# Weight strips and residual tiles moved in two transfers, partitions 0 to 119 and 120 to 127

## The chip, the cores and the metric

The kernel runs on one core of one Trainium2 chip. The metric is the device time of one execution in microseconds (us), as the median of several runs. The profile comes from one further execution, recorded by the hardware profiler. Its engines are TensorE (PE, with its weight loads shown apart as PEld), VectorE (DVE), ScalarE (ACT), GpSimd (POOL) and SyncE (SP), which here issues nearly all data transfers (DMA). A line such as L507 is a line of the kernel.

## The reference, cut to what matters

Four layers in a row on 2048 tokens of width 576: A, B, A, B, each added to its input (the residual) after a layernorm. A is a local attention over 8 dilated positions, with a product with `wqkv` before it and one with `wo` behind it. B is a recurrent attention: it goes through the tokens in segments of 32, and each segment also sees 8 memory rows that the segment before it produced.

```python
def _A_ref(x, wqkv, wo):
    W, dil = (8, 2)                                   # 32 heads of 18
    qkv = ...(x @ wqkv)...
    idx = pos[:, None] - (jnp.arange(W) * dil)[None, :]
    ...                                               # softmax over the 8 positions, times v
    return o @ wo

def _B_ref(x, mem0, Wq, Wk, Wv, Wo, seg_len):         # 32 heads of 128
    mem = mem0
    for s in range(n_seg):                            # 64 segments of 32 tokens
        h = jnp.concatenate([mem, xs], axis=1)
        q, k, v = ...                                 # h times Wq, Wk, Wv
        ...                                           # masked softmax, times v, times Wo
        mem = o[:, :M, :].copy()                      # the next segment needs it
        outs.append(o[:, M:, :])

x = x + _A_ref(_layernorm(x), A_wqkv, A_wo)
x = x + _B_ref(_layernorm(x), B_mem0, B_Wq, B_Wk, B_Wv, B_Wo, B_seg_len)
x = x + _A_ref(_layernorm(x), A_wqkv, A_wo)
x = x + _B_ref(_layernorm(x), B_mem0, B_Wq, B_Wk, B_Wv, B_Wo, B_seg_len)
```

All inputs are bfloat16.

## The kernel before

All four layers run interleaved: while the two B layers (two "lanes", five segments apart) step through their segments, the two A layers work on tiles of 64 tokens ahead of them. A small planner inside the kernel orders the work of every engine when the program is built; its estimates, and not the chip, decide the order. B's weights (`wq`, `wk`, `wv`, `wo`) stay in on-chip memory. A's weights don't fit beside them. They are cut into 12 strips (9 of `wqkv`, 3 of `wo`), and each tile of A fetches all 12 in turn into a ring of three buffers:

```python
self.strips = [dp.tile([P, 5 * 256], BF16, name=f"strip{i}") for i in range(12)]   # in DRAM
tiles("ring", 3, [P, 5 * 256])                                                     # on chip

def wload(self, i, src, rows, col0, n, prio, dep):
    ...
    def fetch(e):
        dma(out=w.t[:, 0:5 * n], in_=self.strips[i][:, 0:5 * n])
    ...
    o = pl.op("SP", 0.9 if k <= COPY else 0.5, gather if k <= COPY else fetch, prio,
              [dep, self.strip_in.get(i)], acq=[w], lat=4.0)
    if k == COPY:     # the third use also writes the packed strip to DRAM, for the later fetches
        self.strip_in[i] = pl.op("SP", 0.5, lambda e: dma(out=self.strips[i][:, 0:5 * n],
                                                          in_=w.t[:, 0:5 * n]), prio, [o], uses=[w])
```

Two of three strips have n = 256 (128 partitions of 2560 bytes, 320 KB), the third has n = 128 (160 KB). A strip's buffer is taken again when TensorE has read it. TensorE reads it here (L570 for `wqkv`, L680 for `wo`), one weight load and one matmul for each of 25 pieces of three strips:

```python
nc.tensor.matmul(ps.t[:, c * T:(c + 1) * T], lhsT=view()[:, kc, w0:w0 + P], rhs=xn.t[:, kc, :],
                 start=(kc == 0), stop=(kc == 4))
```

The output of each A tile, which B's result is added to later, goes to DRAM (L689) and comes back when B reaches it (L715); a tile is 128 partitions of 1280 bytes:

```python
nc.sync.dma_start(out=(self.x1T if layer == 1 else self.x3T)[:, j], in_=xT.t[:])   # store
nc.sync.dma_start(out=b.t[:], in_=src[:, j])                                       # load again
```

The rest of TensorE's work is B: projections to q and k (L832, L835), v (L879), scores (L919 to L929), probabilities times v (L970) and the product with `wo` (L994):

```python
for h in range(4 * k, 4 * k + 4):
    for mb in range(5):
        nc.tensor.matmul(psY.t[...], lhsT=self.wo[:, w0:w0 + P], rhs=self.OT[:, ..., c0:c1], ...)   # L994
```

Of the kernel before, what the change touches and what calls it, by code (L numbers as in the profile page):

```python
# [35 lines left out]
EPS = 1e-5  # L36
NQ = T // 16
CB = (0, 126, 252, 378, 448)


class _Buf:
# [206 lines left out]
class _K:  # L248
# [37 lines left out]
    def setup(self):  # L286
# [19 lines left out]
        nc.gpsimd.memset(epad[:], 1.0)  # L306
        for t_, pat, b0 in ((epad[:, 0:4, :], [[CB[1], 4]], 0), (epad[:, 4, :], [], CB[4])):
            self.sel(t_, pat + [[-AD, AH]], 1, b0, ALU.is_ge, 0.0)
            self.sel(t_, [[-a, n] for a, n in pat] + [[AD, AH]], -1, AD - 1 - b0, ALU.is_ge, 0.0)
        self.sel(epad[:, 0:4, :], [[0, 4], [0, AH]], -1, HPC * AD - 1, ALU.is_ge, 0.0)  # L310
        self.sel(epad[:, 4, :], [[0, AH]], 1, CB[4] - 4 * HPC * AD, ALU.is_ge, 0.0)
        self.epadT = epadT = cp.tile([P, 5, P], BF16, name="epadT")
        et = epadT[0:AH]
        nc.gpsimd.memset(et, 1.0)
        for t_, pat, b0 in ((et[:, 0:4, :], [[CB[1], 4]], 0), (et[:, 4, :], [], CB[4])):
            self.sel(t_, pat + [[1, P]], -AD, b0, ALU.is_ge, 0.0)
            self.sel(t_, [[-a, n] for a, n in pat] + [[-1, P]], AD, AD - 1 - b0, ALU.is_ge, 0.0)
        nc.gpsimd.memset(et[:, 0:4, HPC * AD:P], 0.0)
        nc.gpsimd.memset(et[:, 4, 0:4 * HPC * AD - CB[4]], 0.0)
        self.ma0 = ma0 = cp.tile([AH, AW, 16], F32, name="ma0")  # L320
# [168 lines left out]
    def wload(self, i, src, rows, col0, n, prio, dep):  # L489

        pl, dma = self.pl, self.nc.sync.dma_start
        step, last = rows
        self.strip_n[i] = k = self.strip_n.get(i, -1) + 1
        w = pl.buf("ring") if k else None

        def view():
            return (w.t if k else self.wo[:, i * 1280:(i + 1) * 1280])[:, 0:5 * n].rearrange("p (k n) -> p k n", k=5)

        def gather(e):
            f, v, r, m = src[0:1, col0:col0 + 1], view(), min(P, src.shape[0] - last), min(n, src.shape[1] - col0)
            dma(out=v[:, 0:4, 0:m], in_=bass.AP(f.tensor, f.offset, [[src.shape[1], P], [step * src.shape[1], 4], [1, m]]))
            (dma if k else self.nc.scalar.dma_start)(out=v[0:r, 4, 0:m], in_=src[last:last + r, col0:col0 + m])

        def fetch(e):
            dma(out=w.t[:, 0:5 * n], in_=self.strips[i][:, 0:5 * n])  # L507
        if k == 0:
            o = self.first = pl.op("SP", 0.65, gather, -20.0 + 0.01 * i, lat=4.0)
            return view, (), o  # L510
        o = pl.op("SP", 0.9 if k <= COPY else 0.5, gather if k <= COPY else fetch, prio, [dep, self.strip_in.get(i)], acq=[w], lat=4.0)
        if k == COPY:
            self.strip_in[i] = pl.op("SP", 0.5, lambda e: dma(out=self.strips[i][:, 0:5 * n], in_=w.t[:, 0:5 * n]), prio, [o], uses=[w])
        return view, (w,), o

    def a_tile(self, layer, j, dep, due, span):

        nc, pl = self.nc, self.pl
# [3 lines left out]
        def pr(f):  # L522
            return due - span * (1.0 - f)
        Q = PR[f"A{layer}"]
        if layer == 1:
            xT = pl.buf("x1")
# [8 lines left out]
            b = pl.op("PE", 0.16, tr, pr(0.04), [a], acq=[ps, xT], uses=[x0], mm=5)  # L535
            o_x = pl.op(AD_, _evac(320), lambda e, ps=ps: self.copy(e, xT.t[:], ps.t[:, 0:5 * T].rearrange("p (c t) -> p c t", c=5)),
                        pr(0.05), [b], uses=[ps, xT])
        else:
            xT = self.acc[0][j][0]
# [19 lines left out]
        for part in (0, 1, 2):  # L559
            ps = pl.buf("r")  # L560
            o = o_n
            for c in range(5):
                if c % 2 == 0:
                    n = 256 if c < 4 else P
                    view, w, ow = self.wload(part * 3 + c // 2, self.A_wqkv, (P, 512), part * D + CB[c], n, pr(Q[1]) - PR[f"ring{layer}"], wgate)
                w0 = c % 2 * CB[1]

                def mm(e, c=c, view=view, ps=ps, w0=w0):
                    for kc in range(5):
                        nc.tensor.matmul(ps.t[:, c * T:(c + 1) * T], lhsT=view()[:, kc, w0:w0 + P], rhs=xn.t[:, kc, :],  # L570
                                         start=(kc == 0), stop=(kc == 4))
                o = pl.op("PE", 0.146, mm, pr(Q[1] + 0.03 * part), [o, ow], acq=[ps, dst[part]] if c == 0 else (),
                          uses=[xn, *w] if c == 0 else [xn, *w, ps], lat=0.0 if c < 4 else None, mm=5)
                if c == 0 and part > 0:
                    def hcopy(e, part=part):
# [3 lines left out]
                        else:  # L579
                            self.copy(e, h, hin[0].t[:, part - 1])  # L580
                    got[part, "h"] = pl.op("DVE" if first else ("POOL", "ACT") if early else "POOL", 0.25, hcopy, pr(Q[1]), [o] if first else [o, hin[1]],
                                           uses=[dst[part]] if first else [dst[part], hin[0]])
# [22 lines left out]
        o = None  # L605
        for n, (c0, nb) in enumerate(((0, 2), (2, 2), (4, 1))):
            def prod(e, c0=c0, nb=nb):
                self.tt(e, big.t[:, c0:c0 + nb], qT.t[:, c0:c0 + nb].unsqueeze(2).to_broadcast([P, nb, AW, T]),
                        win(kT.t, c0, nb), ALU.mult)
            o = pl.op(("POOL", "DVE") if early else "POOL", (1.0 * nb + 0.05, 0.15 + 0.3 * nb), prod, pr(Q[2] + 0.02 * n), [o] if o else [got[0], got[1], got[1, "h"]],  # L610
                      acq=[big] if n == 0 else (), uses=[qT, kT] if n == 0 else [big, qT, kT], lk=True)
# [9 lines left out]
        o = o_l = pl.op("PE", 0.29, logits, pr(Q[3]), [o], acq=[psL, e_], uses=[big], mode="C", mm=20)  # L621

        def amax(e):
            v = psL.t[:, 0:P].rearrange("p (w t) -> p w t", w=AW)
            if first:
# [3 lines left out]
        o = pl.op("DVE", 0.6, amax, pr(Q[3]), [o], acq=[nmx], uses=[psL])  # L629
        o = pl.op("ACT", 0.28, lambda e: nc.scalar.activation(out=e_.t[:], in_=psL.t[:, 0:P].rearrange("p (w t) -> p w t", w=AW),  # L630
                                                              func=ACT.Exp), pr(Q[3]), [o], uses=[psL, e_])

        def norm(e):
            nc.vector.tensor_reduce(out=ssum.t[:], in_=e_.t[:].rearrange("p w t -> p t w"), axis=AX.X, op=ALU.add)
            nc.vector.reciprocal(out=ssum.t[:], in_=ssum.t[:])
        o = pl.op("DVE", 0.68, norm, pr(Q[3]), [o], acq=[ssum], uses=[e_])
        o = pl.op("DVE", 0.3, lambda e: self.tt(e, e_.t[:], e_.t[:], ssum.t[:].unsqueeze(1).to_broadcast([P, AW, 16]), ALU.mult),
                  pr(Q[3]), [o], uses=[e_, ssum], lk=True)

        def spread(ps, c0, nb):  # L640
            for c in range(nb):
                for g in range(NQ):
                    q4 = slice(g * AH, (g + 1) * AH)
                    nc.tensor.matmul(ps[g].t[:, c * P:(c + 1) * P], lhsT=self.epadT[q4, c0 + c, :],  # L644
                                     rhs=e_.t[q4].rearrange("p w t -> p (w t)"), start=True, stop=True, skip_group_check=True)
        b = o
        evs = {}
        for n, (c0, nb) in enumerate(((0, 2), (2, 3))):
            ps = [pl.buf("r") for _ in range(NQ)]
            b = pl.op("PE", 0.03 + 0.05 * nb, lambda e, ps=ps, c0=c0, nb=nb: spread(ps, c0, nb), pr(Q[4] + 0.02 * n), [b], acq=ps,  # L650
                      uses=[e_], mode="R", mm=4 * nb)
# [6 lines left out]
        for c0, nb in ((0, 2), (2, 2), (4, 1)):  # L658
# [6 lines left out]
        o = pl.op(PD, (2.6, 0.85), lambda e: self.tt(e, big.t[:, :, 0:4], big.t[:, :, 0:4], big.t[:, :, 4:8], ALU.add),  # L665
                  pr(Q[5] + 0.02), mus, uses=[big], lk=True)
        o = pl.op(PD, (1.44, 0.5), lambda e: self.tt(e, big.t[:, :, 0:2], big.t[:, :, 0:2], big.t[:, :, 2:4], ALU.add),
                  pr(Q[5] + 0.04), [o], uses=[big], lk=True)
        o = o_o = pl.op(PD, (0.78, 0.33), lambda e: self.tt(e, oT.t[:], big.t[:, :, 0], big.t[:, :, 1], ALU.add),
                        pr(Q[5] + 0.06), [o], acq=[oT], uses=[big], lk=True)  # L670
        ps = pl.buf("r")
        for mb in range(5):
            if mb % 2 == 0:
                n = 256 if mb < 4 else P
                view, w, ow = self.wload(9 + mb // 2, self.A_wo, (CB[1], CB[4]), mb * P, n, pr(Q[6]) - PR[f"ring{layer}"], o_l)
            w0 = mb % 2 * P

            def mm(e, mb=mb, view=view, ps=ps, w0=w0):
                for c in range(5):
                    nc.tensor.matmul(ps.t[:, mb * T:(mb + 1) * T], lhsT=view()[:, c, w0:w0 + P], rhs=oT.t[:, c, :], start=(c == 0), stop=(c == 4))  # L680
            o = pl.op("PE", 0.147, mm, pr(Q[6]), [o, ow], acq=[ps] if mb == 0 else (),
                      uses=[oT, *w] if mb == 0 else [oT, *w, ps], lat=0.0 if mb < 4 else None, mm=5)
        if layer == 1 and first:
            for d in self.wo_in:
                pl.after(d, o)
        o = pl.op("DVE", 0.49, lambda e: nc.vector.tensor_tensor(out=xT.t[:], in0=xT.t[:],
                                                                 in1=ps.t[:, 0:5 * T].rearrange("p (c t) -> p c t", c=5), op=ALU.add),
                  pr(Q[6]), [o], uses=[ps, xT])
        xst = pl.op("SP", 0.5, lambda e: nc.sync.dma_start(out=(self.x1T if layer == 1 else self.x3T)[:, j], in_=xT.t[:]),  # L689
                    pr(0.95), [o], uses=[xT])  # L690
        (self.x1_stored if layer == 1 else self.x3_stored)[j] = xst
        xnb = pl.buf(f"xnb{layer}")
# [1 line left out]
        def wr2(e, m, rstd):  # L694
# [5 lines left out]
            for o, i, bc in views:  # L700
                self.tt(e, o, i, bc(m), ALU.subtract)
                self.tt(e, o, o, bc(rstd), ALU.mult)
        o = self.layernorm(xT, o, pr(Q[7]), wr2, 2.5, wacq=[xnb], early=early)
        o = pl.op("ACT", 0.27, lambda e: self.copy(e, xnb.t[64:128, :, 5, :], xnb.t[0:64, :, 4, :]),
                  pr(Q[7]), [o], uses=[xnb])
# [3 lines left out]
    def residual(self, lane, j, dep, prio):  # L709

        nc, pl = self.nc, self.pl
        b = pl.buf(("x3", "x5")[lane])
        xb = pl.buf("fin") if lane == 1 else None
        src = (self.x1T, self.x3T)[lane]
        o = pl.op("SP", 0.5, lambda e: nc.sync.dma_start(out=b.t[:], in_=src[:, j]), prio,  # L715
                  [dep, (self.x1_stored, self.x3_stored)[lane][j]], acq=[b] if xb is None else [b, xb])
        self.acc[lane][j] = (b, o, xb)

# [443 lines left out]
```

## Time and profile before

| what | value |
|---|---|
| time, median of 3 runs | 2142.14 us (2141.03 to 2143.61) |
| span of the profiled execution | 2133.8 us |
| granted TensorE clock | 0.987 of full speed |
| DMA, all queues | 265.14 MB, 124 GB/s on average |
| strips, 320 KB each | 488 transfers, 3.5 us from issue to landing |
| strips, 160 KB each | 244 transfers, 4.0 us |
| residual tiles, stored and loaded | 4 x 32 transfers of 160 KB, 3.9 to 4.5 us |

How to read the profile: the page gives each engine's busy time and its share of the span, and the same in 40 equal slices, as tenths. A view of waits lists, for each engine and line, what ended the idle time before it: another engine's instruction, the landing of a transfer (DMA), or "issue", where no semaphore explains it. Its columns are total us, number of times, longest us. The DMA queues are listed with their packets, megabytes and the share of the 16 DMA engines' time. Beside the packets of the data, queue 8 and queue 14 carry the engines' own instructions[...].

### The profile page before, as it was taken

The numbers are of one execution on the slowest core, as the hardware profiler recorded it, in microseconds if no ns is written. First come the engines' busy times: TensorE is split into PE (matmuls) and PEld (weight loads), VectorE is DVE, ScalarE is ACT, GpSimd is POOL, SyncE is SP. The second block draws the span as 40 slices with busy tenths as digits, with TensorE's granted clock in tenths as the row PEclk, the third lists the DMA queues.
The fourth block names the chain that finished last, engine by engine and source line by source line (L and its number), as shares of the span: only waits on it lengthen the run. The fifth ranks groups of instructions, "written<-read, shape, count | busy, mean of one in ns | idle before, by whom it ended". The sixth has DMA issues, their size and how long they took to land.

```text
span 2133.8 us, 132983 instructions
## 1 busy us (share of the span) xinstructions
PE 2017.4 (95%) x60717; PEld 1732.3 (81%) x60717; DVE 1416.8 (66%) x3754; ACT 1137.8 (53%) x2803; POOL 832.5 (39%) x1289
## 2 busy tenths in 40 slices
PE   1688999999999999999999999999999999999998
PEld 1577888888888888888888888888888888888876
DVE  4477676766666666766766676667667666665565
ACT  1354555555555555555555555555555555655554
POOL 3235434444343344434444443343444334342320
PEclk7899999999999999999999999999999999999999
DMA  9744343343443344334333433334344333331220
GB/s 324 201 148 141 122 127 123 124 138 106 126 127 121 113 124 141 113 117 127 126 116 117 142 121 119 116 127 127 118 128 130 115 117 124 123 121 59 75 76 10
DMA packets 158307, 265.14 MB, mean 124 GB/s; under 512 B 23464, under 2 KB 89904, under 8 KB 157616
## 3 DMA queue, kind: packets, MB, share of 16 engines
q1 hardware_dynamic: 152016, 237.38, 35.5%
q0 software_dynamic: 4576, 18.88, 2.6%
q8 instruction: 474, 7.77, 1.5%
q14 instruction: 89, 0.73, 0.1%
q10 hardware_dynamic: 1152, 0.39, 0.1%
HBM read 240.46 MB, written 16.12 MB: 120 GB/s over the span
## 4 chain that ended last, share of the span: by engine, by line
PE 89%; DMA 6%; issue 2%; DVE 2%; ACT 1%; SPq 0%; ACTq 0%; DVEq 0%
PE r L832 29%; PE r L994 18%; PE r L879 17%; PE r L570 7%; PE r L835 7%; DMA ring<-strip 3%; PE r L970 3%; PE r L680 2%; PE r L644 2%; PE r L470 2%; PE r L929 1%; PE r L919 1%; DMA x<-in_B_mem_dram 1%; PE r L619 1%; PE r L923 1%
## 5 line engine op out<-in xcount | busy, mean ns | idle before, releaser
L832 PE MATMUL r<-hT,wq 128*128 128x80 bf16 (+1 forms) x8832 | 660.3, 198 | 4.6 <-ACT hT L276 2.8
L832 PE MATMUL r<-hT,wk 128*128 128x80 bf16 (+1 forms) x8832 | 662.5, 199 | 1.5 <-issue 1.3
L832 PEld LDWEIGHTS <-wq 128*128 128x128 bf16 x8832 | 500.9, 99 | 47.7 <-issue 35.0
L835 PE MATMUL r<-hT,wqk_r 128*128 128x160 bf16 (+1 forms) x2208 | 507.1, 230 | 0.2 <-issue 0.2
L276 ACT ACTIVATE qk<-r 128x480 bf16<-128x480 f32 (+2 forms) x668 | 351.0, 526 | 265.7 <-PE r L835 254.7
L832 PEld LDWEIGHTS <-wk 128*128 128x128 bf16 x8832 | 447.1, 99 | 1.5 <-issue 1.4
L994 PE MATMUL r<-OT,wo 128*128 128x80 bf16 (+1 forms) x11040 | 418.6, 200 | 27.6 <-issue 22.9
L994 PEld LDWEIGHTS <-wo 128*128 128x128 bf16 x11040 | 394.8, 100 | 39.4 <-issue 34.5
L879 PE MATMUL r<-wv,hT 128*32 128x512 bf16 x5376 | 355.5, 381 | 2.4 <-issue 2.0
L283 POOL TENSOR_TENSOR big<-qT,kT 128x1024 bf16<-128x1024 bf16 x189 | 314.7, 1685 | 60.3 <-ACT kT L276 33.7
L283 POOL TENSOR_TENSOR ex<-ex,sum 128x320 bf16<-128x320 bf16 x138 | 106.9, 775 | 570.7 <-DVE sum L779 509.2
L879 PEld LDWEIGHTS <-hT 128*32 128x32 bf16 x6720 | 173.1, 96 | 127.8 <-issue 5.0
L276 ACT ACTIVATE V<-r 128x512 bf16<-128x512 f32 x305 | 181.4, 596 | 159.2 <-PE r L879 159.1
L835 PEld LDWEIGHTS <-wqk_r 128*128 128x128 bf16 x2208 | 219.7, 99 | 0.5 <-issue 0.4
L768 DVE TENSOR_REDUCE nmx<-r 128x8 f32<-128x320 f32 x276 | 133.3, 483 | 108.6 <-PE r L923 108.4
L276 ACT ACTIVATE OT<-r 128x320 bf16<-128x320 f32 (+1 forms) x378 | 134.4, 423 | 112.3 <-PE r L970 111.7
L570 PE MATMUL r<-xn,ring 128*128 128x64 bf16 x4725 | 176.9, 194 | 15.6 <-DMA ring<-in_A_wqkv_dram 11.6
L570 PEld LDWEIGHTS <-ring 128*128 128x128 bf16 x4725 | 157.4, 98 | 34.5 <-issue 14.1
L276 ACT ACTIVATE big<-r 128x256 bf16<-128x256 f32 (+1 forms) x288 | 109.1, 430 | 89.4 <-PE r L644 88.4
L283 POOL TENSOR_TENSOR xnb<-x,st 128x256 bf16<-128x256 f32 x124 | 64.6, 521 | 205.4 <-DVE st L476 205.4
L1013 DVE CAST hT<-r 128x64 bf16<-128x64 f32 (+1 forms) x68 | 14.9, 219 | 194.9 <-PE r L994 194.8
L769 DVE TENSOR_TENSOR r<-r,nmx 128x320 f32<-128x320 f32 x276 | 137.8, 499 | 9.5
(147 smaller groups left out, 2978.6 us busy)
## 6 DMA issues: line engine op xcount, KB each, us to landing
ring<-strip SPq DMA_DIRECT2D x488, 320.0 KB, 3.5
ring<-strip SPq DMA_DIRECT2D x244, 160.0 KB, 4.0
x1T<-x SPq DMA_DIRECT2D x32, 160.0 KB, 3.9
x<-x1T SPq DMA_DIRECT2D x32, 160.0 KB, 4.1
x3T<-x SPq DMA_DIRECT2D x32, 160.0 KB, 4.5
x<-x3T SPq DMA_DIRECT2D x32, 160.0 KB, 4.5
wo<-in_B_Wo_dram POOLq DMA_DIRECT2D x4, 1152.0 KB, 26.0
wq<-in_B_Wq_dram POOLq DMA_DIRECT2D x2, 2048.0 KB, 20.6
```

The source lines that it names most:

```text
L276: nc.scalar.activation(out=out, in_=in_, func=ACT.Copy, scale=1.0 if scale is None else scale)
L283: (self.nc.vector if e == "DVE" else self.nc.gpsimd).tensor_tensor(out=out, in0=in0, in1=in1, op=op)
L470: nc.tensor.matmul(psf, lhsT=(self.ones if c < 4 else self.ones_h)[:, :], rhs=xs.t[:, c].rearrange("p a t -> p (a t)"), start=(c == 0), st ...
L570: nc.tensor.matmul(ps.t[:, c * T:(c + 1) * T], lhsT=view()[:, kc, w0:w0 + P], rhs=xn.t[:, kc, :], start=(kc == 0), stop=(kc == 4))
L644: nc.tensor.matmul(ps[g].t[:, c * P:(c + 1) * P], lhsT=self.epadT[q4, c0 + c, :], rhs=e_.t[q4].rearrange("p w t -> p (w t)"), start=True, ...
L768: nc.vector.tensor_reduce(out=m, in_=v, axis=AX.X, op=ALU.max, negate=True)
L769: nc.vector.tensor_tensor(out=v, in0=v, in1=m.unsqueeze(len(shp) - 1).to_broadcast(shp), op=ALU.add)
L832: nc.tensor.matmul(pv[:, hh, wi, a:b], lhsT=self.Wb[wi][0][:, kc, h * P:(h + 1) * P], rhs=hT.t[:, kc, a:b], start=(hh == 0 and wi == 0 and ...
L835: nc.tensor.matmul(pv[:, hh, :, a:b], lhsT=self.Wb[0][1][:, h * P:(h + 1) * P], rhs=hT.t[:, 4:6, a:b], start=False, stop=(hh == n - 1), sk ...
L879: nc.tensor.matmul(ps.t[c * 32:(c + 1) * 32, :], lhsT=l, rhs=w, start=(kc == 0), stop=(kc == 4))
L970: nc.tensor.matmul(ps[c].t[:, i * n + a - c0:i * n + z - c0], lhsT=V[b].t[q4, r, i, :], rhs=pt.t[q4, i, b, a:z], start=(i == 0 and b == bl ...
L994: nc.tensor.matmul(psY.t[:, mb * W80 + c0:mb * W80 + c1], lhsT=self.wo[:, w0:w0 + P], rhs=self.OT[:, h % 16 // 4 * 8 + h // 16 * 4 + h % 4 ...
```

## The change

Every transfer of a strip (fetch, and the one-time store of the packed strip) and every store and load of a residual tile is issued as two transfers, one for partitions 0 to 119 and one for 120 to 127. The first gatherings of the strips from the inputs, the loads of x, the stores of the output and the loads of B's weights stay whole. The bytes moved are the same. The planner's estimates aren't touched, so it still counts each pair as one transfer.

What it is for: a transfer is spread over the core's 16 DMA engines. 120 and 8 partitions don't spread over 16 engines as 128 do, so that the frequent transfers load the DMA engines unevenly, and can leave one of them to other traffic.

```diff
+PQU = (slice(0, 120), slice(120, 128))
...
         def fetch(e):
-            dma(out=w.t[:, 0:5 * n], in_=self.strips[i][:, 0:5 * n])
+            for p in PQU:
+                dma(out=w.t[p, 0:5 * n], in_=self.strips[i][p, 0:5 * n])
...
         if k == COPY:
-            self.strip_in[i] = pl.op("SP", 0.5, lambda e: dma(out=self.strips[i][:, 0:5 * n], in_=w.t[:, 0:5 * n]), prio, [o], uses=[w])
+            self.strip_in[i] = pl.op("SP", 0.5, lambda e: [dma(out=self.strips[i][p, 0:5 * n], in_=w.t[p, 0:5 * n]) for p in PQU], prio, [o], uses=[w])
...
-        xst = pl.op("SP", 0.5, lambda e: nc.sync.dma_start(out=(self.x1T if layer == 1 else self.x3T)[:, j], in_=xT.t[:]),
+        xst = pl.op("SP", 0.5, lambda e: [nc.sync.dma_start(out=(self.x1T if layer == 1 else self.x3T)[p, j], in_=xT.t[p]) for p in PQU],
                     pr(0.95), [o], uses=[xT])
...
-        o = pl.op("SP", 0.5, lambda e: nc.sync.dma_start(out=b.t[:], in_=src[:, j]), prio,
+        o = pl.op("SP", 0.5, lambda e: [nc.sync.dma_start(out=b.t[p], in_=src[p, j]) for p in PQU], prio,
                   [dep, (self.x1_stored, self.x3_stored)[lane][j]], acq=[b] if xb is None else [b, xb])
```

## The prediction

> **What bounds the kernel now.** I read the page's parts 1 and 2 first, then the waits of TensorE, then one stall in the timeline, then the DMA queues and the issues of the strips.
>
> ```profile
> PE 2017.4 (95%) x60717; PEld 1732.3 (81%) x60717; DVE 1416.8 (66%) x3754; ACT 1137.8 (53%) x2803; POOL 832.5 (39%) x1289
> ...
> PE   1688999999999999999999999999999999999998
> ```
>
> TensorE is busy from the fifth of 40 slices to the end. What is not matmul there costs time one to one; what delays another engine costs only if TensorE ends up waiting. So I look for TensorE's idle time.
>
> ```profile
> PE r L994 <- issue: 22.9, 34, 1.3
> ...
> PE r L680 <- DMA ring<-strip: 3.6, 9, 0.9
> PE r L570 <- DMA ring<-strip: 3.4, 6, 1.1
> ```
> ```profile
> PEld L832 <- issue: 36.5, 78, 2.9
> PEld L994 <- issue: 34.5, 56, 1.4
> ...
> PEld L570 <- DMA ring<-strip: 5.6, 9, 1.2
> PEld L680 <- DMA ring<-strip: 5.1, 11, 1.0
> ```
>
> The columns are total us, times, longest. Waits for a strip of A's weights are small: about 10 us (weight loads and matmuls tell of the same waits twice). Waits with the releaser "issue", where no semaphore explains the idle time, are larger. Those of L832 mostly sit at the start of a group, right after narrow matmuls, and look like a change of shape; those of L994 sit inside a loop. One of them, in the timeline of TensorE and of the DMA-issuing queue:
>
> ```profile
> 445.06 1.32 PE L994 MATMUL r<-OT,wo 128*128 128x80 bf16 x32
> 447.61 0.88 PE L994 MATMUL r<-OT,wo 128*128 128x80 bf16 x20 [1.23 <-issue]
> ```
> ```profile
> 441.99 1.27 SPq L507 DMA_DIRECT2D ring<-strip  x3
> ```
>
> In the middle of one loop over Wo, with all operands present, TensorE stands still for 1.23 us. Three strips (two of 320 KB, one of 160 KB) had been issued from 441.99 us on.
>
> ```profile
> q1 hardware_dynamic: 152016, 237.38, 35.5%
> ...
> q8 instruction: 474, 7.77, 1.5%
> ```
>
> Queue 8 carries instructions: 474 packets of 7.77 MB / 474 = 16.4 KB. TensorE has 60717 weight loads and as many matmuls; 121434 / 474 = 256 instructions per packet. In the trace's list of packets the one before this stall starts at 445.19 us and lasts 1.05 us: it ends at 446.24, and the next matmul is at 447.61. So this stall is a wait for instructions.
>
> I counted this over the steady part (130 to 2085 us). Gaps of over 150 ns at every 256th TensorE instruction sum to 43.5 us beyond a usual 50 ns. From the instruction 320 places earlier, the earliest place from which a fetch never starts sooner than about 1 us later, to the packet's start: 1.43 us in the median for the 91 pages fetched while queue 1 moved nothing, 2.54 us for the 257 with over 100 of its packets in that time. Packets themselves take much the same, 0.98 and 0.96 us. The fetch stands in line behind the strips. The 91 quiet pages cost 1.7 us of stalls in all; the 173 with under 60 packets beside them 3.5 us; the 287 others 40.0 us.
>
> The reverse shows too. A strip's landing is told by 16 increments of its semaphore, one for each DMA engine. For the 454 strips whose increments can be told apart, the 15th comes 3.25 us after the issue in the median, the 16th 3.64 us; in 183 of them the last is over 0.4 us behind the 15th, while the 15th is within 0.23 us of the 14th in nine of ten. One engine alone lags, by about the length of a fetch.
>
> [...] The longer wait beside strips fits a shared engine, but its 1.1 us is more than one turn of a 2560-byte packet (0.10 us in the packet list).[...]
>
> **The change part by part.** Order of work on TensorE, VectorE, ScalarE and GpSimd stays the same instruction for instruction, as both programs' listings show; only waits and DMA issues differ.
>
> (a) Removed: if the engine left out is the fetching one, strips and residual tiles no longer delay fetches. Other loads still use it (x and out, 72 KB each, 64 issues). If every page behaved like the quiet ones, 474 x 1.7 us / 91 = 9 us would remain of 43.5; busy pages lie more often in the dense code (PV followed by Wo), so I keep 5 to 12 us: minus 31 to 38, taken as minus 35 us.
>
> (b) Moved: landings of strips. Without the lagging engine a strip lands with its 15th increment; against that its second part is issued about 0.43 us later (0.38 us median duration of an issue in the listing of the strips, plus the space between two), and each following strip of a group of three 0.43 and 0.86 us later than now. I replayed the 732 strips with their recorded issue times, first weight loads and 15th increments, the second part landing 2.7 us after its issue. Stalls on strips go from 9.9 to 6.7 us: minus 3 us. Now 5 in 100 second and third strips land within 0.1 us of their use, but these are the late ones, 4.7 to 5.0 us after the issue, that waited on the lagging engine.
>
> (c) Added on TensorE: the first weight load on a strip waits for two DMA semaphores instead of one. Listed waits beyond one per instruction go from 66 to 798, so 732 more wait instructions. Steady pairs on the ring come every 29 ns, each weight load starting 2 ns after the matmul before. A wait instruction in the trace holds back what follows by about 15 ns (matmul at +15 behind a wait at 0). Estimate from these: 732 x 0.016 = plus 12 us, if none is hidden. They also add 732 / 256 = 3 pages.
>
> (d) Added on the issuing queue: DMA copies go from 997 by some 870, x 0.43 = 375 us of SyncE, which has 520 us of records in 2134, waits included. Not on the path. A DMA also waits for the one eight issues before it, now only four strips back. Before, 10 in 100 issues come within 6.4 us of that landing; I allow 2 us.
>
> Sum: -35 - 3 + 12 + 2 = -24 us, thus 2142 - 24 = 2118 us.
>
> **The rivals.** First, another engine carries the fetches. Then (a) is gone[...]. The same replay with 16th increments kept gives 36.4 us of strip stalls instead of 9.9. Sum: 26.5 + 12 + 2 + 3 = plus 43 us, 2185 us. For it speaks that nothing in the trace names the engine; against it, that a lagging engine exists and the cut at 120 leaves out exactly one. I give it 2 in 10. Second, fetches wait for something that all engines share[...]. Then the quiet pages are quick for that reason and a split changes nothing: (b) without most of the lag, (c) and (d), plus 10 to 25 us. One lagging engine speaks against it. Third, extra waits on TensorE are free, hidden behind the 29 ns of a matmul: then 2105 us; or each holds back the early weight loads by a whole pair, 732 x 0.03 = 22 us, 2128 us. Fourth, everything works and the freed time is taken by waits for ScalarE and VectorE behind it: their share is 53% and 66%, so I expect little of it.
>
> **Range and chances.** With the right engine 2100 to 2130, otherwise 2155 to 2190. 8 in 10: 2097 to 2172. 2% is 43 us: over 2% faster (under 2099) needs free waits and nearly all fetch stalls gone, 0.13. Over 2% slower (above 2185) needs the wrong engine and the upper half of its sum, 0.10. The rest 0.77.
>
> **What would show it.** Right: the "issue" waits of L994 (34.5 and 22.9 us above) fall by more than half while those of L832 stay; fetch packets start about 1.4 us after their place throughout; the last increment of a strip's first part no longer lags; one of the first part's 16 increments comes at the issue, the other 15 with the data. Wrong: "issue" waits as before, or waits of L570 and L680 for strips above 20 us, or matmul pace at the strips' first use clearly over 16 ns slower. If the time falls and "issue" waits don't, my reason is wrong even where the number fits.

## The result and the profile after

The changed kernel takes 2204.53 us (2200.21 to 2209.72) against 2141.59 us: a ratio of 1.0297, 95% interval 1.0266 to 1.0327. It is 63 us slower, where the prediction had it 24 us faster and its range ended at 2172.

The page's part 1, with the queues of part 3 and two lines of the issues:

```profile
PE 2041.7 (93%) x60717; PEld 1741.3 (79%) x60717; DVE 1417.7 (64%) x3754; ACT 1139.6 (52%) x2803; POOL 835.1 (38%) x1289
...
q1 hardware_dynamic: 158120, 237.40, 39.0%
...
q8 instruction: 477, 7.82, 1.6%
...
ring<-strip SPq DMA_DIRECT2D x488, 300.0 KB
...
ring<-strip SPq DMA_DIRECT2D x488, 20.0 KB
```

The work is the same, matmul for matmul. Queue 1 has 6104 more packets, and they are 4-byte ones that tell of landings: 872 pairs times 7, that is 15 + 8 instead of 16 for each transfer that was cut. The semaphore of a part rises once some 0.5 us after the issue began and then 15 or 8 times with the data, from 2.8 us on (medians); that of a whole strip before rises 16 times, from 2.5 us on. And of the data packets of queue 1, in the steady part (130 to 2085 us of both traces), the number under way at once that lasts longest is 16 before (197.6 us in all) and 15 after (232.1 us). I read this as 15 DMA engines for 120 partitions and 8 for 8, with one increment from each; the trace gives no engine's number. Queue 1 moves the same data, but its packets now take 39.0% of the 16 engines' time instead of 35.5% of a shorter span. The waits of TensorE (total us, times, longest), matmuls and then weight loads:

```profile
PE r L996 <- issue: 44.3, 54, 2.2
...
PE r L572 <- DMA ring<-strip: 14.0, 22, 2.0
```
```profile
PEld L996 <- issue: 61.3, 73, 2.3
PEld L834 <- issue: 37.5, 81, 2.9
...
PEld L572 <- DMA ring<-strip: 11.6, 19, 2.0
...
PEld L682 <- DMA ring<-strip: 3.9, 8, 0.7
```

(Lines have moved by two: L996 is the L994 of before, L834 the L832, L572 the L570.) The waits without a releaser inside the loop over Wo, which should have fallen by more than half, nearly doubled: 34.5 to 61.3 us. Those of L834 stayed, as said. Waits for strips at L572 more than doubled. One of the stalls, in the timelines of TensorE and of the issuing queue:

```profile
499.88 2.47 PE L996 MATMUL r<-OT,wo 128*128 128x80 bf16 x64
503.71 1.46 PE L996 MATMUL r<-OT,wo 128*128 128x80 bf16 x36 [1.37 <-issue]
```
```profile
497.12 1.43 SPq L509 DMA_DIRECT2D ring<-strip  x4
498.64 0.49 SPq L741 DMA_DIRECT2D out_dram<-x  x1
499.50 0.68 SPq L509 DMA_DIRECT2D ring<-strip  x2
500.27 0.66 SPq L691 DMA_DIRECT2D x1T<-x  x2
```

It is the picture of before: transfers are issued, the 16384-byte instruction packet starts behind them at 501.14 us, takes 1.09 us, and TensorE goes on 1.48 us after its end.

Both programs have the same 60717 matmuls in the same order, so the two traces can be laid over each other and each gap between two matmuls compared. I sort the differences in the steady part into gaps at every 256th instruction ("page"), gaps before a matmul on the ring ("ring") and the rest. The 72.4 us between the spans of the two profiled executions (the medians of the timed ones lie 63 us apart) are page +50.3, ring +18.9, other +3.8, start -0.5. So TensorE waits for its own instructions, the very thing that was to be cured, and in second place for strips.

### The profile page after: what moved, and what is told of

It is laid out like the page before. It is cut to its first block, busy times and chain, and to the rows that moved or that the text cites. A ratio compares the mean times of both kernels' runs of the same rounds, so it can differ in the third digit from the quotient of the medians.

```text
span 2206.2 us, 134717 instructions
## 1 busy us (share of the span) xinstructions
PE 2041.7 (93%) x60717; PEld 1741.3 (79%) x60717; DVE 1417.7 (64%) x3754; ACT 1139.6 (52%) x2803; POOL 835.1 (38%) x1289
## 4 chain that ended last, share of the span: by engine, by line
PE 83%; DMA 10%; issue 4%; DVE 1%; SPq 1%; ACT 1%; POOL 0%; ACTq 0%; DVEq 0%; POOLq 0%
PE r L834 27%; PE r L996 17%; PE r L881 15%; DMA ring<-strip 7%; PE r L572 6%; PE r L837 6%; PE r L972 3%; PE r L682 2%; PE r L646 1%; PE r L471 1%; PE r L931 1%; PE r L921 1%; DMA ring<-in_A_wqkv_dram 1%; DMA x<-in_B_mem_dram 1%; PE r L621 1%
## 5 line engine op out<-in xcount | busy, mean ns | idle before, releaser
L834 PE MATMUL r<-hT,wq 128*128 128x80 bf16 (+1 forms) x8832 | 660.8, 198 | 5.8 <-ACT hT L277 2.7
L834 PE MATMUL r<-hT,wk 128*128 128x80 bf16 (+1 forms) x8832 | 662.7, 199 | 1.6 <-issue 1.6
L834 PEld LDWEIGHTS <-wq 128*128 128x128 bf16 x8832 | 501.2, 99 | 48.3 <-issue 35.6
L996 PE MATMUL r<-OT,wo 128*128 128x80 bf16 (+1 forms) x11040 | 421.1, 200 | 50.8 <-issue 44.3
L834 PEld LDWEIGHTS <-wk 128*128 128x128 bf16 x8832 | 447.4, 99 | 2.0 <-issue 1.9
L996 PEld LDWEIGHTS <-wo 128*128 128x128 bf16 x11040 | 396.3, 100 | 65.0 <-issue 61.3
L881 PE MATMUL r<-wv,hT 128*32 128x512 bf16 x5376 | 361.3, 384 | 3.5 <-issue 3.2
L572 PE MATMUL r<-xn,ring 128*128 128x64 bf16 x4725 | 185.8, 194 | 34.1 <-DMA ring<-in_A_wqkv_dram 14.2
L572 PEld LDWEIGHTS <-ring 128*128 128x128 bf16 x4725 | 161.5, 98 | 57.8 <-issue 26.9
## 6 DMA issues: line engine op xcount, KB each, us to landing
wo<-in_B_Wo_dram POOLq DMA_DIRECT2D x4, 1152.0 KB, 26.5
```

Of the source, the lines that this page charges most:

```text
L834: nc.tensor.matmul(pv[:, hh, wi, a:b], lhsT=self.Wb[wi][0][:, kc, h * P:(h + 1) * P], rhs=hT.t[:, kc, a:b], start=(hh == 0 and wi == 0 and ...
L881: nc.tensor.matmul(ps.t[c * 32:(c + 1) * 32, :], lhsT=l, rhs=w, start=(kc == 0), stop=(kc == 4))
L996: nc.tensor.matmul(psY.t[:, mb * W80 + c0:mb * W80 + c1], lhsT=self.wo[:, w0:w0 + P], rhs=self.OT[:, h % 16 // 4 * 8 + h // 16 * 4 + h % 4 ...
```

## The experiments

All are timed beside the kernel before on the same chip; a ratio comes from runs of the two kernels taken in turn and can differ a little from the quotient of two medians. "Page" and "ring" are us against the kernel before, in the profiled executions. They are one execution each, and the span of such an execution differs from that before by up to 10 us more or less than the timed runs do, so amounts of a few us say little. "Fetch wait" is from the place 320 instructions earlier to the instruction packet's start, median, where over 100 packets of queue 1 ran beside it; "instr. packet" is the median duration of a 16384-byte packet. The last column is a mean over the steady part; a dash: no packets of 2560 bytes there.

```text
run          ratio (95% interval)       page   ring  fetch wait  instr. packet  2560-byte packets
before       1                             0      0    2.55 us      0.96 us          130.5 ns
after        1.0297 (1.0266-1.0327)    +50.3  +18.9    2.84         1.14             145.1
a_alone      1.0222 (1.0183-1.0262)    +38.6   +2.0    2.73         1.12             143.2
w112_alone   0.9995 (0.9981-1.0010)     -0.0   -1.5    2.41         1.09             136.2
dummy8       0.9954 (0.9940-0.9968)    -15.1   +9.3    2.34         1.01             133.9
spacer1      0.9948 (0.9933-0.9963)    -15.0   +7.6    2.31         0.98             132.1
s104_24      1.0360 (1.0321-1.0399)    +13.9  +53.9    2.57         1.09             136.5
s88_40       1.0343 (1.0301-1.0385)    +32.6  +40.1    2.52         1.06             133.4
s64_64       1.0369 (1.0343-1.0394)     -8.0  +79.3    2.10         1.09             138.4
cols2        0.9996 (0.9970-1.0021)    -36.1  +30.6    1.96         1.02             -
rows2        1.0054 (1.0033-1.0074)     +1.7  +18.3    2.64         0.96             -
cols2_plan   1.0228 (1.0199-1.0257)   (another order of work)  1.96  1.01            -
resid_only   1.0031 (1.0017-1.0044)     +4.7   +5.6    2.63         0.98             131.8
mid_split    0.9966 (0.9954-0.9978)    -16.7   +8.8    2.25         0.99             135.2
```

**Which half of the change costs: the 120 partitions, or the second transfer?**

```diff
-PQU = (slice(0, 120), slice(120, 128))          # a_alone: strips only; residual tiles whole
+PQU = (slice(0, 120),)
+PQX = (slice(0, 128),)                          # used for the residual tiles in place of PQU
```

> Strips are fetched for partitions 0 to 119 only, in one transfer each (partitions 120 to 127 keep what they had, so the output is not the reference's); residual tiles whole as before. Number of transfers and of TensorE's waits as before. Theory S (shape): 120 partitions over fewer engines make packets slower and hold the fetching engine longer; then most of the loss is here, 2170 to 2200 us, and the gaps at every 256th TensorE instruction stay near the 99 us of the changed kernel (before: 47 us). Theory P (pairing): the second transfer does it; then 2135 to 2150 us and about 47 us of gaps.

2175.8 us against 2133.88. This kernel leaves the strips' last 8 partitions unloaded. With as many transfers as before and 6% fewer bytes on the strips, 38.6 of the 50.3 us of page gaps are already there, and the ring hardly changes. Theory S holds for these gaps: beside strips a fetch waits 2.73 us instead of 2.55, and its packet takes 1.12 us instead of 0.96. The waits of TensorE's matmuls and of its weight loads in this run (L997 is the loop over Wo):

```profile
PE r L997 <- issue: 38.8, 50, 2.0
```
```profile
PEld L997 <- issue: 51.6, 68, 2.1
```

The counterpart keeps whole strips and adds a second transfer:

```diff
+        self.junk, self.slot = wp.tile([P, 640], BF16, name="junk"), 0                     # dummy8
...
             dma(out=w.t[:, 0:5 * n], in_=self.strips[i][:, 0:5 * n])
+            self.slot = (self.slot + 8) % P
+            dma(out=self.junk[self.slot:self.slot + 8, 0:640], in_=self.strips[i][120:128, 0:640])
```

> Strips whole as before, and beside each a transfer of 8 partitions of 1280 bytes into a spare buffer that nobody reads. Theory P (pairing: the second issue, its packets and the later issue of the following strips): 2175 to 2205 us, gaps at every 256th instruction well above 47 us. Theory S (shape): 2140 to 2155 us, gaps about 47 us, waits for strips up by a few us because each following strip is issued 0.3 to 0.6 us later.

2124.87 us, faster than before, which neither theory had. The ring got 9.3 us worse, as the later issues would do it; but the page gaps fell by 15.1 us. A second transfer of 8 partitions by itself is thus not what makes the fetches late. The gain needed a run of its own:

```diff
-            self.slot = (self.slot + 8) % P
-            dma(out=self.junk[self.slot:self.slot + 8, 0:640], in_=self.strips[i][120:128, 0:640])
+            self.slot = (self.slot + 1) % P                                                # spacer1
+            dma(out=self.junk[self.slot:self.slot + 1, 0:64], in_=self.strips[i][127:128, 0:64])
```

> Strips whole, and behind each a transfer of one partition of 128 bytes into a spare buffer that nobody reads: it loads the engines with next to nothing and only makes the next strip's issue some 0.3 us later. If the gain of the run with 8 spare partitions (43.5 to 29 us of gaps, time 0.995 of before) comes from spacing, it is the same here or a little more: gaps 25 to 32 us, 2115 to 2128 us. If it came from anything that the 8 engines' packets do, this run is at 2134 us.

2124.09 us, page -15.0: the same gain with a transfer that moves 128 bytes. It fits the spacing: within a group of three the next strip is issued 0.75 us after the one before it instead of 0.41 to 0.49 us (medians), which leaves fewer strips in front of a fetch; its wait falls from 2.55 to 2.31 us.

**Which engine fetches?**

```diff
-PQU = (slice(0, 120), slice(120, 128))
+PQU = (slice(0, 104), slice(104, 128))          # s104_24
+PQU = (slice(0, 88), slice(88, 128))            # s88_40
```

> Both parts moved, cut at 104 instead of 120[...]. Theory E (the fetching engine is one of those that 120 partitions use and 8 do not): if it is 13 or 14, the last increment of the first part no longer lags while a fetch runs (0.72 of cases in the changed kernel), gaps at every 256th instruction fall under 15 us, and the time is 2100 to 2130 us. If it is 8 to 12, the lag stays and the time is 2200 to 2240 us[...].

> Cut at 88[...]. Theory E: if the fetching engine is 11 to 14, gaps at every 256th instruction fall under 15 us, but strips land later (12 packets per engine instead of 8, about 0.4 us more per strip), waits for strips 30 to 60 us: 2130 to 2180 us. If it is 8 to 10 everything gets worse, over 2230 us.

2205.87 and 2203.68 us. Queue 1 has 159864 and 156376 packets, 872 x 9 and 872 x 5 more than before, so 25 and 21 of its 4-byte packets tell of a pair's landing instead of 16 for a whole transfer. With equal shares that fits 13 + 12 engines (8 and 2 packets of data on each) and 11 + 10 (8 and 4). The numbers of single engines in the two expectations are an assumption that no trace shows. Read as asked, both answers are "neither": the lag of the last increment became rarer, as if the fetch were on one of the freed engines now and then. So I took only the transfers with exactly one fetch beside them, numbered the fetches, and counted by the number modulo 8 how often the last increment came over 0.3 us behind the one before it:

```text
fetch number modulo 8             0      1      2      3      4      5      6      7
after, part of   8 partitions   57/57   4/42   7/42   4/39  13/37   8/31   3/34  35/40
s88_40, part of 40 partitions   50/53  45/50  10/48   8/44  14/50  10/53  10/55  40/41
s104_24, part of 104            19/22  19/21  23/27  20/20  13/17   8/31   4/31  18/18
after, part of 120              33/33  29/33  29/30  32/34  28/36  26/30  33/35  23/30
```

There is no one fetching engine: the lag comes and goes with the fetch's number, in a cycle of eight (part of 8 partitions: 57 of 57 at place 0 and 35 of 40 at place 7, at most 13 of 37 elsewhere). I read it as successive fetches that go round several engines. By this reading, of the eight places in the cycle two are on engines that 8 partitions use, three on those of 40, six on those of 104, and all eight on those of 120. The engine that the change leaves out carries none of them. The two parts not shown fit in: in that of 88 partitions the places 7, 0, 1 and 2 lag, in that of 24 those and 3. Since each larger set only adds places, at least six different engines take part; whether 7 and 0, or 5 and 6, share one stays open. In s88_40 the stalls show it by the same number: fetches 3 to 6, whose engines carry neither part of a strip, wait 2.23, 1.85, 1.77 and 1.69 us and cost 2.8, 5.3, 2.6 and 2.5 us of stalls; fetches 7, 0 and 1 wait 2.44, 2.81 and 3.07 us and cost 15.4, 21.5 and 17.7 us (fetch 2 lies between, 2.67 us). Freeing engines works for the fetches on them; it loads the others, and with 11 and 10 engines in use the strips come late as well.

**Is it the number 15, or other rows per engine?**

```diff
-PQU = (slice(0, 120),)
+PQU = (slice(0, 112),)                          # w112_alone
```

> Strips fetched for partitions 0 to 111 only, one transfer each (112 to 127 keep what they had, so the output is not the reference's). [...] 12.5% fewer bytes than whole. Theory S1 (any number of partitions that gives the engines other rows than whole transfers do makes packets slow): mean of the 2560-byte packets 140 ns or more (before 130.5, 120 alone 143), fetch packets 1.1 us, gaps at every 256th TensorE instruction 65 to 90 us, 2150 to 2175 us. Theory S2 (it is the number of 15 engines): mean about 130 ns, fetch packets 0.97 us, gaps 35 to 43 us, 2125 to 2135 us, as there are fewer bytes.

2132.03 us, with the strips' last 16 partitions left unloaded. Queue 1 has 140112 packets, 744 x 16 fewer than before, as many as the rows left out of 732 fetches and 12 stores. So 16 packets still tell of each landing, which I read as 16 engines with 7 packets of a strip on each. By the instruction packets (1.09 us) S1 is nearer, by the gaps and the time S2; the mean of the 2560-byte packets, 136 ns, lies between. A reading that fits both is that packets are a little slower here too, but what a strip puts on one engine is one packet shorter, and the fetch waits less. The means hide how the packets differ: half of those of 2560 bytes take 102 ns in every run. Over 130 ns take 13 to 19% of them where strips keep 128 partitions, 24 to 26% with the cuts at 64, 88, 104 and 112, and 38 and 40% with 120. So every cut of the strips by partitions has more slow packets, with 16 engines in use (112, 64) too, and 120 the most. Instruction packets go the same way: 1.06 us or more in every run that cuts the strips by partitions, 1.02 us or less where strips keep 128. Why is not settled, and no run here separates one cause from another.

**What does a fetch wait for?** A transfer's share is here what it puts on one engine, 8 packets for a whole strip (128 packets over 16). First as many transfers as in the changed kernel, with 16 engines in both parts by the count of landing packets (165968 packets on queue 1, 872 x 16 more than before); then cuts that keep all 128 partitions.

```diff
-PQU = (slice(0, 120), slice(120, 128))
+PQU = (slice(0, 64), slice(64, 128))            # s64_64
```

> Both parts moved, strips and residual tiles, cut at 64: 16 engines and 4 partitions each in both parts; as many transfers as the changed kernel has. Theory G (a fetch gets its turn between two transfers' shares, so smaller shares let it in sooner, and later issues thin out the queue): gaps under 30 us, waits for strips about 20 us, 2115 to 2135 us. Theory S1: the first 64 partitions have other rows per engine than whole transfers, so packets slow down as with 120: gaps 70 us or more, 2180 to 2205 us.

2214.17 us, above what either theory said, and not for the reason that S1 gave: fetches wait 2.10 us and page gaps fall by 8.0 us, although an instruction packet takes 1.09 us. The loss is the ring, +79.3 us. An issue took 0.587 us in the median here instead of 0.32 in the changed kernel, so the strips of a group start 1.2 to 1.3 us apart instead of 0.76. From its issue to its landing a part takes 3.2 to 3.3 us, no longer than whole strips before (3.5 to 4.0), so the later issues are the likely cause; no run separates them. Theory G is nearer on the gaps (some 35 us; it said under 30) and wrong on the sum.

```diff
-            dma(out=w.t[:, 0:5 * n], in_=self.strips[i][:, 0:5 * n])
+            for c in range(0, 5 * n, 640):       # cols2
+                dma(out=w.t[:, c:c + 640], in_=self.strips[i][:, c:c + 640])
```

> The 320 KB strips moved as two transfers of all 128 partitions, halves of the columns (packets of 1280 bytes), residual tiles whole. Rows per engine as before. Theory G: packets as fast as the 1280-byte ones before (60 ns), gaps at every 256th instruction under 30 us (before 43.5), waits for strips up by 5 to 10 us, 2115 to 2130 us against 2134. Theory P (more transfers cost time by themselves): 2150 us or more.

2130.91 us, no difference that can be measured. Inside, two large amounts cancel: page -36.1, ring +30.6. The weight loads' waits in this run (L995 and L571 are the loops over Wo and wqkv):

```profile
PEld L571 <- DMA ring<-strip: 24.4, 33, 3.2
...
PEld L681 <- DMA ring<-strip: 11.2, 22, 1.3
...
PEld L995 <- issue: 10.6, 25, 0.8
```

Of 34.5 us at Wo 10.6 are left, and the page gaps are 6.8 us in all. Waits for strips are 35.6 us instead of 10.7. To separate the size of packets from that of a transfer's share, the same packets in one transfer:

```diff
-        self.strips = [dp.tile([P, 5 * 256], BF16, name=f"strip{i}") for i in range(12)]
+        self.strips = [dp.tile([P, 2, 672], BF16, name=f"strip{i}") for i in range(12)]    # rows2
...
+        def two(t):
+            return t[:, 0:5 * n].rearrange("p (a b) -> p a b", b=640)
...
-            dma(out=w.t[:, 0:5 * n], in_=self.strips[i][:, 0:5 * n])
+            dma(out=two(w.t), in_=self.strips[i][:, 0:n // P, 0:640])
```

> The 320 KB strips stay one transfer each, but their rows lie in DRAM as two pieces of 1280 bytes with 64 bytes between them, so that each engine's share is 16 packets of 1280 bytes instead of 8 of 2560. As many transfers, issues and waits as before; residual tiles whole. Theory G1 (a fetch waits until the whole share of a transfer on its engine is through): share and wait as before or 8% longer, gaps at every 256th instruction 40 to 55 us, 2130 to 2145 us. Theory G2 (it waits for single packets, so their size counts): gaps near the 7 us of the column halves, without their waits for strips, 2095 to 2110 us.

2152.86 us against 2139.62; the queue and the weight loads' wait:

```profile
q1 hardware_dynamic: 215504, 237.38, 36.6%
```
```profile
PEld L997 <- issue: 38.2, 57, 1.8
...
PEld L573 <- DMA ring<-strip: 16.6, 28, 3.6
```

63488 more packets than before, nearly all of them on the strips, whose data comes in as many packets of 1280 bytes as in cols2; and yet fetches wait 2.64 us and the gaps stay. That speaks for G1, a fetch that is let in between the shares of two transfers and not between two packets of a share. The lengths of the shares agree, as estimates from the mean packets of 1280 bytes: in cols2 8 of 67.5 ns, 0.54 us, where a fetch beside strips waits some 0.56 us longer than the 1.4 us of a quiet one; in rows2 16 of 66.6 ns, 1.07 us, where it waits some 1.2 us longer. Waits for strips alone don't hide the fetches either: here the ring costs 18.3 us more and the page gaps stay. The time is above what G1 said. An issue took 0.549 us in the median here instead of 0.382, so the strips of a group start 0.62 to 0.66 us apart instead of 0.41 to 0.49, which is part of why they land later. By spacer1 such a spacing should have shortened the gaps a little; why it did not stays open.

**What is left of the loss, and a better version.**

```diff
-            for p in PQU:
+            for p in (slice(0, 128),):           # resid_only: strips whole, their one-time store too
                 dma(out=w.t[p, 0:5 * n], in_=self.strips[i][p, 0:5 * n])
```

> Only the residual tiles (128 of the 872 pairs) moved as 120 and 8 partitions, strips whole. By their share of the pairs and by the strips' part of the loss: plus 2 to 10 us over before, that is 2136 to 2144 us against 2134; the gaps at every 256th instruction 44 to 52 us.

2147.13 us against 2139.62: the residual tiles' part is about 7 us of the 63, and the rest is the strips', if the two parts add.

```diff
-        o = pl.op("SP", 0.9 if k <= COPY else 0.5, gather if ..., lat=4.0)
+        o = pl.op("SP", 0.9 if k <= COPY or n > P else 0.5, gather if ..., lat=4.0)    # cols2_plan
```

> Column halves as in the run of that name, with the kernel's planner told that such a pair takes SyncE 0.9 us instead of 0.5. Theory: the 30.6 us that the column halves lost again are waits for strips which the planner issues in groups it believes shorter; if it knows the time it places A's products later and those waits fall to 5 to 15 us while the gaps stay under 10 us: 2105 to 2120 us. If the waits come from elsewhere, about 2130 us as without it. A different plan may also shift the time by some us for reasons of its own.

2192.09 us, a miss. The planner made another order for all engines; page gaps stayed small (18.8 us) but waits that were not there before appeared. The first lines of TensorE's waits:

```profile
PE r L681 <- DVE oT L283: 17.2, 4, 5.2
PE r L571 <- DVE xn L283: 16.9, 1, 16.9
PE r L470 <- ACT xs L464: 14.5, 9, 6.2
PE r L470 <- DVE nma L628: 14.3, 19, 0.8
```

The planner's other constants were found for the old durations. Whether retuned ones would keep the gain of cols2 wasn't tried.

```diff
-            dma(out=w.t[:, 0:5 * n], in_=self.strips[i][:, 0:5 * n])
+            h = 640 if i % 3 == 1 else 5 * n     # mid_split
+            for c in range(0, 5 * n, h):
+                dma(out=w.t[:, c:c + h], in_=self.strips[i][:, c:c + h])
```

> Only the middle strip of each group of three (the second 320 KB one) moved as two column halves; strips and residual tiles otherwise whole. Theory (a fetch waits for one whole share of a transfer, and later issues delay what comes behind them): the first strip is not delayed, the second's second half and the third by about 0.45 us instead of up to 0.9. Against before: gaps at every 256th instruction minus 12 to 22 us (splitting both took 36), waits for strips plus 5 to 12 us (30.6 with both), so minus 5 to 15 us. If the shares don't matter and only the total delay does, minus 3 to plus 3.

2125.74 us against 2132.88. As expected: nearly half of the gain in gaps for under a third of the cost. It, dummy8 and spacer1 (0.9966, 0.9954 and 0.9948; their intervals overlap) are faster than the kernel before by 0.3 to 0.5%.

## Why the prediction was wrong, point by point

- **Bound and cause of the stalls: right.** TensorE sets the time, its gaps at every 256th instruction are waits for instruction fetches, and these stand behind strips. Thinner queues (spacer1) and smaller shares (cols2) shrink them, from 43.5 to 29.0 and 6.8 us.
- **Step (a), "if the engine left out is the fetching one", failed**, and with it the sign: -35 us forecast, page +50.3 measured. "One engine alone lags" was true of each transfer, and I took it for the same engine each time. Increments carry no engine's number, so the trace before could not tell; several engines in turn give the same picture. Leaving out an engine that carries no fetch takes nothing away, and what the transfers became instead makes it worse: beside strips a fetch waits 2.84 us instead of 2.55 and its packet takes 1.14 us instead of 0.96.
- **The first rival had the engine wrong too** ("another engine carries the fetches"), and its sum of +43 us only looks near: it put 26.5 us on strips and 3 (an estimate) on fetches. Measured are 18.9 and 50.3. What it lacked is that moving 120 partitions by itself delays the fetches: a_alone has +38.6 us, with more slow packets and 8 packets per engine as before. No step of mine asked whether 120 partitions move as fast per engine as 128.
- **Step (b), strips: -3 us forecast, ring +18.9 measured.** Without a freed lagging engine nothing pays for the later issues. By the place in the group of three, gaps over 150 ns before a strip's first matmul (whatever ended them) sum to 9.9, 4.5 and 2.5 us before and 10.7, 9.9 and 11.6 us after: what is added grows along the group, as the 0.43 and 0.86 us of that step would have it.
- **Step (c), 732 wait instructions: +12 us forecast, none measured.** From the last matmul on one strip to the first on the next it is 29 ns in the median with one wait and with two. The third rival's first half, that these waits are free, was right.
- **Step (d), further issues: +2 us allowed.** Nothing can be told apart from what (b) holds and the +3.8 us of "other".
- **What I set the wait against.** I compared the 1.1 us that a fetch waits longer beside strips (2.54 us against 1.43) with one packet of 2560 bytes and called it too long. I didn't compare it with a strip's share on one engine: 8 packets times the mean of 130.5 ns is 1.04 us, an estimate close to the 1.1 us. rows2 (16 packets of 1280 bytes in a share, wait 2.64 us, page +1.7) and cols2 (8 of them, wait 1.96 us, page -36.1) fit a wait for whole shares.

## What to carry to other kernels

This program's 121434 TensorE instructions came in 474 packets, 256 in each, and a packet's fetch waited 2.54 us beside strips against 1.43 us while queue 1 moved nothing. The gaps at every 256th instruction summed to 43.5 us; in another program they can be added up in the same way. Here it helped to keep the transfers beside the fetches short per engine or a little apart, as long as the later issues did not cost as much in waits for the data (cols2 gained nothing in the end, mid_split 0.3%). Before a transfer is cut by partitions, measure one part alone. With the strips cut by columns (cols2) the instruction packets stayed at 1.02 us, where every cut of the strips by partitions had 1.06 or more. And when something lags "once per transfer", find out whether it is the same thing each time before building on it.

## What the runs showed of the hardware that I had not expected

Whether a transfer's last increment lags goes by the number of the instruction fetch beside it, in a cycle of eight (57 of 57 against 3 of 34 lagging in the changed kernel); I read it as fetches that go round at least six DMA engines. Transfers of 120 partitions have more slow packets than those of 128: 38 to 40% of those of 2560 bytes take over 130 ns instead of 14%, while half take 102 ns in both. Instruction packets take 1.09 to 1.14 us in the runs with strips of 120, 112 or 64 partitions instead of 0.96. An issue of 64 partitions took 0.59 us, in the changed kernel one of 120 or 8 took 0.32 and 0.30. And some 0.3 us more between two strips' issues, bought with a transfer of 128 bytes that nobody needs, made the kernel 0.5% faster.
